# DeltaNet and MLP kernel: the first chunk's triangular inverse with 64-wide products and predicated evictions, later key norms read from the diagonal of K K^T, and an order planner that knows the port shared by VectorE and GpSimd

## The chip, the core and the metric

The kernel runs on one core of one Trainium2 chip. The metric is the device time of one execution in microseconds; lower is better. The engines are named as in the profile: PE (TensorE; PEld is its weight load), DVE (VectorE), ACT (ScalarE), POOL (GpSimd) and SP (SyncE, which here only issues DMAs). A name such as L841 is line 841 of the kernel before, unless the text says that it is the kernel after.

## The reference

Batch 4, 8 heads, 768 tokens, head size 48, all in float32. The first block is a delta-rule recurrence, the second a layer norm and a two-layer MLP with a residual:

```python
k_n = k / (np.linalg.norm(k, axis=-1, keepdims=True) + 1e-06)
state = np.zeros((B, H, D, D))
for t in range(S):
    y[:, :, t] = einsum('bhd,bhde->bhe', q[:, :, t], state)
    v_old = einsum('bhde,bhd->bhe', state, k_n[:, :, t])
    state = state + bt * einsum('bhd,bhe->bhde', k_n[:, :, t], v[:, :, t] - v_old)
...
x = y.transpose(0, 2, 1, 3).reshape(B, S, H * D)          # H * D = 384
xn = (x - mean) / sqrt(var + 1e-06) * g_ln
out = x + maximum(xn @ w_ch1, 0) @ w_ch2                  # 384 -> 1536 -> 384
```

The MLP weights are float64 in memory and are converted on the chip.

## The kernel before

**Tiling.** The sequence is cut into 12 chunks of C = 64 tokens, for all 32 (batch, head) pairs at once; two batches lie on each half of the 128 partitions. For a chunk, `gram` (L962) computes K K^T on TensorE, `queries` (L970) computes the masked product of q and k, and an inverse of a 64 x 64 unit triangular matrix per head (built from beta, the norms and K K^T) turns the recurrence into products. `recur` (L1127) multiplies it by v (for chunk 0 at L1173), scales the result to u (L1179), makes the output y (L1199), updates the state (L1209), and goes through the layer norm (`bn_stats` L1240, the root L1246, `xln` L1252) and a transpose (L1261) to xnt (L1265). `mlp(c)` (L1284) then does 12 first products of three k-tiles each (L1294), the relu eviction on ACT (L1302), the second product (L1310), the residual add to o on DVE (L1319) and the write.

**Three ways to the inverse.** Chunk 0 uses `first_inverse` (L813), doubling on TensorE: stage n multiplies a masked part of the scaled gram matrix with the inverse so far (product E, L876), evicts it, multiplies again (product Z, L893), transposes (L898) and copies back (`odd_back`, L801). It works on 32-column halves: four stages (n = 1 to 4) for the diagonal blocks of 32, whose masks are multiplied in beforehand (L860, seven on POOL and one on DVE), and a closing pair of products for the corner block (L906, L911). Its two halves of the heads, g = 0 and 1, alternate. Chunk 1 uses `rows_inverse` (L994) with blocks of FB = 16: it is a forward substitution on DVE, 15 steps of a multiply (L1025) and a subtract (L1030) with n * w elements, then a write of the result to memory (xd), eight loads into xt, and two joins of blocks on TensorE (`blocks_join` L1043, `join` L1078). Later chunks go in pairs through `rows_inverse` with blocks of BK = 32 and one `join`.

**Norms.** Chunk 0 has `first_norms`. For later chunks `norms` (L1112) squares k on ACT (L1115), reduces on DVE (L1116), takes three roots on ACT (L1117, L1120), adds 1e-6 on POOL (L1124) and scales v on POOL (`scale_v`, L773).

**Weights.** They come in 12 pieces through five buffers; `convert` (L656) takes each through ACT (L668, L683), DVE (shift L673, mask L678), POOL (multiply L688) and DVE (L700). The buffer of a piece is free for the next fetch after L700.

**Blocks.** `load_blocks` (L609) loads k or q of one chunk in eight DMAs of 32 x 32 blocks, `turned` (L930) transposes them on DVE (L933). `prep_g(m)` (L1390) does this for k of chunks 2m and 2m+1 and computes their grams.

**The order of the work.** Every operation is entered as a `Step` with an engine, a cost estimate and the keys that it reads and writes. `Line.run` (L204) simulates the engines with these costs and lists the steps; `emit` writes them in that order, and each engine executes its instructions strictly in it. DMAs stand in the order of the queue that issues them (SP, ACT or POOL). `pr` is a step's priority, `due` the wanted time of an MLP product; `PATIENCE` is how long an engine may be kept idle for an urgent step. The order is thus fixed when the kernel is built: a step that is late on the chip holds up all behind it on its engine.

Of the kernel before, what the change touches and what calls it, by code (L numbers as in the profile page):

```python
# [59 lines left out]
class Step:  # L60
    __slots__ = (
        "eng", "cost", "fn", "deps", "pr", "lag", "bulk", "start", "end", "n", "users", "name", "t0", "np", "arr", "hold", "ready", "least", "due"
# [3 lines left out]
class Line:  # L66
# [3 lines left out]
    HOP, GIVE, PATIENCE, SLACK, EAGER = 0.17, 0.1, 1.5, 3.0, 0.0  # L70
# [11 lines left out]
    def add(self, eng, cost, fn, r=(), w=(), pr=0.0, lag=0.0, bulk=None, name="", t0=0.7, after=(), np=0, arr=0.0, hold=None, due=None):  # L82
# [3 lines left out]
        s.hold, s.due = False, due  # L86
        deps = set()
# [100 lines left out]
    def foresee(self, now):  # L188

        soon, ends = {e: [] for e in ENGS}, {}  # L190
        for s in self.held:
            if s.start is not None:
                if s.end is not None:
                    ends[s] = s.end
                continue
            t = max(s.t0, now, s.least)
            for d in s.deps:
                z = d.end if d.end is not None else ends.get(d, now)
                t = max(t, z + (0.03 if d.eng == s.eng and d.bulk is None else self.HOP))
            ends[s] = t + s.cost + (self.PE_TAIL if s.eng == "PE" else 0.0)  # L200
            soon[s.eng].append((t, s))
        self.soon = {e: sorted(v, key=lambda x: x[0])[:6] for e, v in soon.items()}

    def run(self):  # L204
# [9 lines left out]
        self.held = [s for s in self.steps if s.hold]  # L214
        self.foresee(0.7)
# [3 lines left out]
        free = {e: 0.7 for e in ENGS}  # L219
# [9 lines left out]

        while todo:  # L230
            best = None
            for e in ENGS:
                for rd, s in self.avail[e]:
                    t = max(free[e], rd)
                    if s.bulk is not None:
                        x = lane(s, e)
                        if x is None:
                            continue
                        t = max(t, x)
                    if best is None or t < best[0]:  # L240
                        best = (t, e)
# [6 lines left out]
            for rd, s in self.avail[e]:  # L248
                if rd <= t + 1e-9:
                    if s.bulk is not None:  # L250
                        x = lane(s, e)
                        if x is None or x > t + 1e-9:
                            continue
# [14 lines left out]
            first = [max(r, t + 0.1) for r, h in self.soon[e] if h.start is None and h.pr < pick.pr]  # L268
# [11 lines left out]
            s.start = t  # L280
            todo -= 1
# [60 lines left out]
def kernel(  # L342
# [77 lines left out]
    masks = [sb(f"m{i}", [128, C], FP32 if i else I32) for i in range(6)]  # L420
    mask4 = sb("mask4", [128, BK], I32)
    xor, bits = sb("xor", [128, C], I32), sb("bits", [128, C], I32)
    eye = sb("eye", [128, BK])
    bm = sb("bm", [128, 2])
# [21 lines left out]
    gds = [dram.tile([128, GH, C], FP32, name=f"gd{i}") for i in range(NG)]  # L446
# [31 lines left out]
    def c_pool(fn, cost, w, r=(), pr=-200, **kw):  # L478
        add("Pool", cost, fn, r, w, pr=pr, hold=False, **kw)

    def c_dve(fn, cost, w, r=(), pr=-200, **kw):
        add("DVE", cost, fn, r, w, pr=pr, hold=False, **kw)

    for i in (0, 2, 1, 3):
# [4 lines left out]
    esx = pts[1]  # L489
    nought = esx.rearrange("p h t -> p (h t)")  # L490
    c_dve(lambda: nc.vector.memset(nought[:, 0:128], 0.0), 0.2, [("esx", 0), ("esx", 1)], pr=-300)
# [10 lines left out]
        lambda: nc.vector.tensor_scalar(  # L502
            out=xb[:, 0, 0:1].bitcast(I32), in0=xor[:, 0:1], scalar1=5, scalar2=1,
            op0=ALU.logical_shift_right, op1=ALU.bitwise_and,
        ),
        0.15, ["bma"], ["xor"],
    )
    for b in range(2):
        c_dve(
            lambda b=b: nc.vector.tensor_scalar(  # L510
                out=bm[:, b : b + 1], in0=xb[:, 0, 0:1].bitcast(I32), scalar1=b, scalar2=None, op0=ALU.is_equal
            ),
            0.15, [("bm", b)], ["bma"], pr=-199,
        )
    c_dve(
# [8 lines left out]
        lambda: nc.vector.tensor_scalar(out=flat[:, 960:992], in0=xor[:, 0:BK], scalar1=BK - 1, scalar2=None, op0=ALU.bitwise_and),  # L524
        0.17, ["eyx"], ["xor"],
    )
    c_dve(
        lambda: nc.vector.tensor_scalar(out=eye, in0=flat[:, 960:992], scalar1=0, scalar2=None, op0=ALU.is_equal),
        0.17, ["eye"], ["eyx"],
    )  # L530
    MPR = [-200, -200, -199, -198, -197, None, -196]
    for n in (0, 1, 2, 3, 4, 6):
        k_, m, w = min(n, 4) if n == 6 else n, masks[n] if n < 6 else mask4, C if n < 6 else BK
        t1, t2 = (flat[:, BK + C * i : BK + C * i + w] for i in (2 * n, 2 * n + 1))
# [4 lines left out]
            0.17, [("ma", n)], ["xor"], pr=MPR[n],  # L539
        )  # L540
        c_dve(
            lambda t2=t2, k_=k_, w=w: nc.vector.tensor_scalar(
                out=t2, in0=bits[:, 0:w], scalar1=k_, scalar2=1, op0=ALU.logical_shift_right, op1=ALU.bitwise_and
            ),
            0.18, [("mb", n)], ["bits"], pr=MPR[n],
# [5 lines left out]
            0.22, [("mask", n)], [("ma", n), ("mb", n)], pr=MPR[n],  # L551
        )
    MASK_SCRATCH = [(x, n) for x in ("ma", "mb") for n in (0, 1, 2, 3, 4, 6)] + ["bma", "eyx"]
    xc = us.rearrange("p h d -> p (h d)")[:, 0 : GH * BK].rearrange("p (h t) -> p h t", t=BK)
    c_pool(
        lambda: nc.gpsimd.tensor_copy(out=es, in_=eye[:, None, :].to_broadcast([128, GH, BK])),
        0.62, [("es", 0), ("es", 1)], ["eye"],
    )
# [72 lines left out]
    ON_DVE = ((1, 1),)  # L631
# [24 lines left out]
    def convert(i, c0=0, n=WN, **kw):  # L656
# [17 lines left out]
            wk, hk, **kw,  # L674
# [799 lines left out]
```

## Time and profile before

| what | value |
|---|---|
| median of 3 runs | 607.21 us (606.29 to 609.96) |
| the profiled execution's own time | 608.22 us |
| its span, first to last instruction | 606.5 us |
| mean granted TensorE clock | 0.946 |
| first MLP product (L1294) starts | 68.26 us |
| first E product of chunk 0's doubling (L876) starts | 15.45 us |
| first product with v (L1173) starts | 52.96 us |
| POOL mask multiplies (L860) | 7, 9.9 us |
| row result of chunk 1 written (xd) | 73.34 us |

The page of a profile gives, in its first part, the busy time and share of each engine; in its second the span in 40 equal slices, a digit being the busy share in tenths, with the granted TensorE clock below in the same tenths. A line of a list of waits reads "engine, tile and line, <- what ended the wait: us in total, times, longest". A line of the timeline starts with its start and its length in us. In a table of windows, each engine has busy us and, in brackets, instructions; at the end stand the clock, the DMA share and GB/s. A group line ends with busy us, mean ns of one, and the idle time before it with what ended it.

### The profile page before, as it was taken

To read this page: it belongs to the slowest core of one execution; us is meant where nothing else is said; L and a number is where in the kernel's file an instruction comes from. 1 tells how busy PE (TensorE), PEld (TensorE's weight loads), DVE (VectorE), ACT (ScalarE), POOL (GpSimd) and SP (SyncE) were. 2 spreads that over 40 slices of the span, in tenths; PEclk is the share of its full clock that TensorE was granted. 3 is DMA by queue.
4 is the path that set the end of the run, shared out by engine and by line. 5 is a ranking of instruction groups with operands and counts; after the bars stand their busy time and mean duration, and the time that the engine had idled before them with its cause. 6 is when DMAs were issued, how large, how long until landed. Compare 5 with 4: busy or idle time off the path is not lost.

```text
span 606.5 us, 20389 instructions
## 1 busy us (share of the span) xinstructions
PE 556.4 (92%) x9118; PEld 414.8 (68%) x9118; DVE 315.0 (52%) x709; ACT 171.9 (28%) x406; POOL 125.0 (21%) x164
## 2 busy tenths in 40 slices
PE   7855886999999999799989899998999999999996
PEld 4744665668678667568758577767768678677773
DVE  7876987994145981236970327951349814210000
ACT  5554564112142202232203223203314023221010
POOL 7784165623303130013130010100010000100000
PEclk9555697999999999999999999999999999999999
DMA  8981378877346343137243245031340030010101
GB/s 188 271 151 20 118 210 167 139 115 131 55 116 126 53 70 79 29 102 132 41 65 78 39 119 98 14 79 19 86 89 16 14 85 4 2 27 0 27 0 26
DMA packets 160039, 48.49 MB, mean 80 GB/s; under 512 B 151112, under 2 KB 154320, under 8 KB 159952
## 3 DMA queue, kind: packets, MB, share of 16 engines
q1 hardware_dynamic: 154064, 42.65, 33.5%
q0 software_dynamic: 2720, 3.96, 4.0%
q8 instruction: 71, 1.16, 0.8%
q10 hardware_dynamic: 3168, 0.59, 0.6%
q14 instruction: 16, 0.13, 0.1%
HBM read 33.93 MB, written 13.24 MB: 78 GB/s over the span
## 4 chain that ended last, share of the span: by engine, by line
PE 77%; DVE 11%; ACT 4%; issue 3%; DMA 3%; SPq 2%; ACTq 0%; DVEq 0%
PE ffa L1294 20%; PE ffa L1310 18%; PE ffb L1310 10%; PE ffb L1294 9%; PE two L950 3%; SPq L475 2%; PE ffb L1094 2%; PE by L1199 2%; DVE tmp L1025 2%; DVE xb L1030 2%; PE ffb L1089 2%; PE by L1139 2%; PE two L1192 2%; PE two L1209 1%; PE by L1261 1%
## 5 line engine op out<-in xcount | busy, mean ns | idle before, releaser
L1294 PE MATMUL ffa<-xnt,w_sb 128*128 128x256 f32 x600 | 148.8, 392 | 4.6 <-DVE o L1319 3.3
L1310 PE MATMUL ffa<-w_sb,h_all 128*128 128x384 f32 x384 | 146.0, 494 | 1.0 <-ACT h_all L1302 0.6
L1294 PEld LDWEIGHTS ffa<-xnt,w_sb 128*128 128x128 f32 x600 | 112.9, 194 | 29.1 <-DVE o L1319 7.3
L1310 PEld LDWEIGHTS ffa<-w_sb,h_all 128*128 128x128 f32 x384 | 70.1, 190 | 43.8 <-ACT h_all L1302 2.3
L1310 PE MATMUL ffb<-w_sb,h_all 128*128 128x384 f32 x192 | 79.2, 494 | 4.7 <-ACT es L1099 2.8
L1302 ACT ACTIVATE h_all<-ffa 128x256 f32<-128x256 f32 x100 | 35.7, 381 | 166.5 <-PE ffa L1294 112.0
L1294 PE MATMUL ffb<-xnt,w_sb 128*128 128x256 f32 x264 | 65.2, 383 | 1.7 <-ACT es L1099 1.4
L1030 DVE TENSOR_TENSOR xb<-xb,tmp 128x60 f32<-128x60 f32 (+19 forms) x170 | 60.6, 357 | 5.8
L1025 DVE TENSOR_TENSOR tmp<-xb,gb 128x60 f32<-128x60 f32 (+19 forms) x170 | 58.3, 343 | 4.0
L475 POOL DMA_DIRECT2D tb<-in_k_dram x80 | 52.2, 659 | 39.1 <-DVE kt L933 31.3
L1294 PEld LDWEIGHTS ffb<-xnt,w_sb 128*128 128x128 f32 x264 | 49.2, 190 | 10.5 <-ACT es L1099 2.0
L1310 PEld LDWEIGHTS ffb<-w_sb,h_all 128*128 128x128 f32 x192 | 35.0, 190 | 28.0 <-ACT es L1099 4.8
L1124 POOL TENSOR_SCALAR knrm<-knrm 128x16 f32<-128x16 f32 x11 | 3.7, 337 | 234.5 <-ACT knrm L1120 227.1
L1104 DVE COPY xt<-ffb 32x512 f32<-32x512 f32 x22 | 15.0, 684 | 53.3 <-PE ffb L1089 24.4
L1302 ACT ACTIVATE h_all<-ffb 128x256 f32<-128x256 f32 x44 | 16.9, 384 | 67.5 <-PE ffb L1294 61.3
L1082 DVE STREAM_TRANSPOSE xnj<-xt 128x512 f32<-128x512 f32 x11 | 7.8, 710 | 49.8 <-DMA xt<-xd 28.3
L1319 DVE TENSOR_TENSOR o<-ffa,x 128x384 f32<-128x384 f32 x16 | 8.8, 556 | 41.7 <-PE ffa L1310 37.0
L1319 DVE TENSOR_TENSOR o<-ffb,x 128x384 f32<-128x384 f32 x8 | 4.4, 552 | 41.2 <-PE ffb L1310 35.3
L688 POOL TENSOR_TENSOR words<-words,x 128x768 f32<-128x768 f32 (+1 forms) x11 | 20.0, 1821 | 21.3 <-ACT xnt L1265 8.8
L1099 ACT ACTIVATE es<-ffb 32x512 f32<-32x512 f32 x22 | 13.0, 589 | 38.0 <-DVE xt L1104 18.3
L933 DVE STREAM_TRANSPOSE qt<-tb 128x1024 f32<-128x1024 f32 x10 | 12.4, 1240 | 16.5 <-PE two L950 16.5
L1116 DVE TENSOR_REDUCE ksum<-xln 128x16 f32<-128x768 f32 x11 | 10.4, 949 | 19.2 <-ACT xln L1115 19.2
(169 smaller groups left out, 648.9 us busy)
## 6 DMA issues: line engine op xcount, KB each, us to landing
words<-in_moe_w_ch_dram SPq DMA_DIRECT2D x10, 768.0 KB, 5.8
gd<-gsb SPq DMA_DIRECT2D x11, 512.0 KB, 3.5
v<-in_v_dram SPq DMA_DIRECT2D x24, 192.0 KB, 3.9
kr<-in_k_dram SPq DMA_DIRECT2D x48, 96.0 KB, 3.3
out_dram<-o SPq DMA_DIRECT2D x48, 96.0 KB, 2.2
tb<-in_k_dram POOLq DMA_DIRECT2D x40, 64.0 KB, 3.3
gb<-gd SPq DMA_DIRECT2D x40, 64.0 KB, 3.7
tb<-in_q_dram SPq DMA_DIRECT2D x40, 64.0 KB, 2.9
```

Source lines behind the costliest of these rows:

```text
L475: add(eng, cost, lambda: QUEUE[eng].dma_start(out=out_, in_=in_), r, w, bulk=n * ns / 16e3, **kw)
L688: lambda: nc.gpsimd.tensor_tensor(out=lo.bitcast(FP32), in0=lo.bitcast(FP32), in1=esc.bitcast(FP32), op=ALU.mult),
L933: lambda: nc.vector.transpose(dst.rearrange("p i (u t) -> p i u t", t=BK), tb[i].rearrange("p (h u d) -> p h u d", u=2, d=BK)),
L950: nc.tensor.matmul(p_g[half(e ^ (hp & n)), hp, g * NP + j], kt[drows(hp), l], rt[drows(hp), i])
L1025: nc.vector.tensor_tensor(out=t, in0=xv[:, 0:n, j : j + 1].to_broadcast([128, n, w]), in1=gv[:, j : j + 1, j + 1 : L].to_broadcast([128, n ...
L1030: nc.vector.tensor_tensor(out=rest, in0=rest, in1=t, op=ALU.subtract)
L1099: add("ACT", act(512), lambda rows=rows: nc.scalar.mul(es[rows], p[rows], -1.0), [ATT[1]], [("es", e)], **kw)
L1104: "DVE", dve(512), lambda rows=rows: nc.vector.tensor_copy(out=xt[rows, :, BK:C], in_=p[rows]),
L1294: nc.tensor.matmul(p[:, 0:TOK], w1_sb[:, t, f * 128 : (f + 1) * 128], xnt[:, t], start=(t == 0), stop=(t == KC - 1))
L1302: "ACT", act(256), lambda hk=hk, p=p: nc.scalar.activation(h_all[:, hk], p[:, 0:TOK], ACTF.Relu),
L1310: lambda f=f, g=g, p=p, hk=hs[f]: nc.tensor.matmul(p[:, 0:DM], h_all[:, hk, g * 128 : (g + 1) * 128], w2_sb[:, f], start=(f == 0), stop=(f ...
L1319: lambda o=o, p=p, g=g: nc.vector.tensor_tensor(out=o, in0=p[:, 0:DM], in1=x[:, g], op=ALU.add),
```

## The change

1. `first_inverse` works on all 64 columns, in five stages (n = 1 to 5) and no closing pair. Product E (L851 after) multiplies the scaled gram matrix as it is, without a mask, with the transposed inverse so far. Its eviction is a `copy_predicated` on DVE (L859 after): only the elements that stage n's mask keeps are written, over an identity matrix that stands in the buffer beforehand. Product Z (L855 after) of that with the inverse so far is the new inverse; DVE transposes it (L866 after), and ACT copies it back in three pieces (L822 after; in the last stage one of the three is on DVE, L820 after).
2. POOL writes these six identity buffers before (L556 after, two copies of 512 each). They lie in buffers that chunks 1 to 3 use later (kt, two gsb, two xt, pt). The POOL mask multiplies are gone; there is one mask more (n = 5) to build on DVE.
3. The row steps of chunk 1's `rows_inverse` (blocks of 16) are on POOL; those of later chunks stay on DVE.
4. `norms` no longer squares and reduces: two DMAs on SP read the diagonal of K K^T of the chunk from memory (1024 single elements each), one root follows on ACT (L1064 after). For this the gram buffers in memory have one row more.
5. `prep_g(1)` loads its blocks (chunks 2 and 3) through SP instead of POOL; later ones stay on POOL.
6. The planner: steps carry `port`; a step of DVE isn't started while a POOL step with which it would share the port runs, and the other way round. PATIENCE is 0.8 instead of 1.5, the estimate of coming steps counts when an engine is free, and the MLP products' due times after chunk 0 are 6 us later. `hold=False` of the constants' helpers is dropped; `add` doesn't use the argument.

In the order that comes out, the DVE instructions of the doubling stand among the weight conversions as before; the transposes of k for chunks 2 and 3 (L873 after) stand ahead of chunk 0's xln; on TensorE the q transposes and `queries` of chunk 1 stand ahead of the transposes of xln; on ACT the root of chunk 1's norms stands between the two layer-norm roots of chunk 0. On SP, counted from the weight piece that SP issued at 14.13 us in the profile before, 51 DMAs stand ahead of the write of chunk 1's row result (the last of the moved block loads is the 41st); before there were 35.

```diff
-    HOP, GIVE, PATIENCE, SLACK, EAGER = 0.17, 0.1, 1.5, 3.0, 0.0
+    HOP, GIVE, PATIENCE, SLACK, EAGER = 0.17, 0.1, 0.8, 3.0, 0.0
...
+        s.port = port if eng != "Pool" else 1 if bulk is not None else port or 2
...
+            if s.port:
+                until, kind = ports["Pool" if e == "DVE" else "DVE"]
+                if kind + s.port > 2:
+                    t = max(t, until)
...
+    BEGIN = [(kts[2], "kt", 2), (gsbs[2], "g", 2), (gsbs[3], "g", 3), (xts[2], "xt", 2), (xts[3], "xt", 3), (pts[1], "pt", 1)]
+    for t, *key in BEGIN:
+        for g in range(2):
+            c_pool(
+                lambda t=t, g=g: nc.gpsimd.tensor_copy(out=t[:, g * H : g * H + H], in_=eye[:, None, :].to_broadcast([128, H, C])),
+                0.65, [(*key, x) for x in range(2)], ["eye"],
+            )
...
+        for n in range(1, 6):
+            ep, ekey = paired(BEGIN[n][0]), tuple(BEGIN[n][1:])
+            for g in range(2):
...
+                        nc.tensor.matmul(pe_[half(e), hp, j], gs[a, hp, j], xnj_[a, hp, j])
...
+                        nc.tensor.matmul(px[half(e ^ hp), hp, j], ep[half(e), hp, j], xt[half(e), 2 * j + hp])
...
+                    "DVE", 0.75,
+                    lambda i=i, n=n, ep=ep: nc.vector.copy_predicated(
+                        ep[:, :, i], masks[n][:, None, None, :].to_broadcast(shape), pe_[:, :, i]
+                    ),
...
+                if n < 5:
+                    add("DVE", dve(512), lambda i=i: nc.vector.transpose(xnj_[:, :, i], px[:, :, i]), Z, [("qt", 1, g)], **kw)
+                back(g, px, Z, ("ACT", "ACT", "ACT") if n < 5 else ("ACT", "DVE", "ACT"))
...
+        eng = nc.gpsimd if L < BK else nc.vector
...
-                nc.vector.tensor_tensor(out=rest, in0=rest, in1=t, op=ALU.subtract)
-
-            add("DVE", 2 * dve(n * w), row, gbk, ["xb"], **kw)
+                eng.tensor_tensor(out=rest, in0=rest, in1=t, op=ALU.subtract)
+
+            if L < BK:
+                add("Pool", 2 * (0.28 + 1.9e-3 * n * w), row, gbk, ["xb"], **kw)
+            else:
+                add("DVE", 2 * dve(n * w), row, gbk, ["xb"], port=1, **kw)
...
-        add("ACT", act(768), lambda: nc.scalar.square(ksq, kr), raw_keys(c), KSQ, **kw)
-        add("DVE", dve(768), lambda: nc.vector.tensor_reduce(out=ksum[i], in_=ksq, axis=AXX, op=ALU.add), KSQ, [("ks", i)], **kw)
...
+            own = flat[e * C * w : e * C * w + C * (w + 1)].rearrange("(s x) -> s x", x=w + 1)[:, 0:w:C]
+            dma("SP", ksum[i][half(e)], own, GH * C, 11, [("gd", c % NG)], [("ks", i, e)], **kw)
...
+        add("ACT", 0.22, lambda: nc.scalar.sqrt(knrm[i], ksum[i]), [("ks", i, e) for e in range(2)], kk, **kw)
...
-        return 42.0 + 42.2 * c + 1.35 * t - (14.0 if c else 0.0)
+        return 42.0 + 42.2 * c + 1.35 * t - (8.0 if c else 0.0)
...
-            load_blocks(2 * (c % 2), k, c, "Pool", pr=pr, t0=40.0 * m if m > 1 else 18.0)
+            load_blocks(2 * (c % 2), k, c, "Pool" if m > 1 else "SP", pr=pr, t0=40.0 * m if m > 1 else 18.0)
```

## The prediction

> **What bounds the kernel now.** I read the page first, then the windows by stage, the PE waits in the worst stage, and the timeline there. The page:
>
> ```profile
> span 606.5 us, 20389 instructions
> ...
> PE 556.4 (92%) x9118; PEld 414.8 (68%) x9118; DVE 315.0 (52%) x709; ACT 171.9 (28%) x406; POOL 125.0 (21%) x164
> ...
> PE   7855886999999999799989899998999999999996
> ...
> PEclk9555697999999999999999999999999999999999
> ```
>
> TensorE is the bound, but not from the start: its idle 50.1 us and its half clock lie mostly in the first eight slices (15.2 us each). By stage (PE busy is the second number):
>
> ```profile
> core 0: us, PE busy (x) PEld busy (x) DVE busy (x) ACT busy (x) POOL busy (x), PEclk, DMA share, GB/s
> 0.00:15.45 15.45, 11.77 (x163) 7.58 (x163) 11.57 (x48) 9.01 (x19) 11.91 (x27) 0.90 0.90 189
> 15.45:52.96 37.51, 23.94 (x717) 21.54 (x716) 27.57 (x51) 21.80 (x58) 25.70 (x30) 0.50 0.81 176
> 52.96:68.26 15.30, 9.49 (x207) 8.10 (x207) 12.42 (x41) 7.49 (x14) 4.50 (x4) 0.50 0.02 3
> 68.26:120.00 51.74, 43.69 (x1054) 33.72 (x1055) 44.06 (x78) 22.41 (x40) 29.30 (x29) 0.91 0.80 182
> 120.00:606.50 486.50, 467.49 (x6981) 343.80 (x6979) 219.40 (x495) 111.22 (x276) 53.63 (x76) 1.00 0.31 61
> ```
>
> The cuts are the first product of the doubling (15.45), the product with v (52.96), the first MLP product (68.26). So: 13.6 us idle in the doubling, 5.8 in the tail to the MLP, 8.1 in the middle, 19.0 later. After 68.26 TensorE has about 507 us of full-clock work (538.2 minus 27.1 idle minus 4.5 lost to half clock at 68.3 to 70.5 and 97.9 to 104.7). That work doesn't shrink, so **the change is worth the earlier MLP start plus the later stalls that it takes away**. Why the doubling is slow:
>
> ```profile
> PE two L876 <- ACT pt L880: 4.4, 2, 4.2
> PE by L893 <- ACT u L811: 4.0, 2, 2.7
> ```
>
> ```profile
> 12.04 2.33 DVE L841 COPY_PREDICATED es<-m,gsb 128x256 f32<-128x256 int32 x2
> 27.68 2.25 DVE L673 TENSOR_SCALAR words<-words 128x384 uint32<-128x384 uint32 x1
> 28.21 1.49 POOL L777 TENSOR_TENSOR v<-v,knat 128x768 f32<-128x768 f32 x1
> 35.35 1.14 PE L950 MATMUL ffb<-qt,kt 48*64 48x64 f32 x32
> 42.15 3.12 DVE L673 TENSOR_SCALAR words<-words 128x768 uint32<-128x768 uint32 x1
> ```
>
> ACT is named, but ACT's copy stood behind DVE: the L673 op takes 0.35 us alone (23.65) and 2.25 or 3.12 beside Pool work. A copy_predicated of 256 takes 0.45 alone, 1.08 and more beside Pool's mask multiply (L860).
>
> **What the Trainium skill says.** "GPSIMD Engine Reference", 8. Key points: GpSimd shares its SBUF interfaces with VectorE and contends with DVE instructions in a 2-port mode or with two SBUF inputs; the trace agrees (0.35 against 2.25). "TensorE: Matmul & The Clock Gate", Part 1: the clock is half or full, by activity over windows of about 3.4 us; here 1.00 to 12.5 us, 0.50 until 70.5. "DMA: Bandwidth & Descriptors", Why small descriptors are slow: a fixed cost per packet; the new norm transfers are 1024 elements of 4 bytes each, which no run here shows.
>
> **The change, part by part.**
>
> *Before the doubling.* Pool writes 12 identity copies of 512 (L556 shows one: 0.62), 7.4 us, about 5.4 to 14. They may delay the DVE norm chain (9.05 to 10.3): 0 to 2, I take 0.5. Against it the identity products (L849, 2 x 1.22) go, which stood before the first E. E of group 0 then starts at the end of the gram of chunk 1 (14.4) plus 0.5: about 15.0.
>
> *Doubling.* Before: four stages of E, Z with 32 columns (1.08 per 32 products) plus two 32-wide closing products per half. After: five stages, 4 x 32 products of 64 columns each. Price: the L950 row, 1.14 at half clock (the width costs 0.06, since the row of 32-wide ones is bound by issue). 20 x 1.14 = 22.8; four transposes and query halves between them, 4 x 1.11 = 4.4: 27.3 us of TensorE. DVE per stage: two predicated evictions from PSUM and two transposes of 512:
>
> ```profile
> L1082 DVE STREAM_TRANSPOSE xnj<-xt 128x512 f32<-128x512 f32 x11 | 7.8, 710 | 49.8 <-DMA xt<-xd 28.3 <-PE ffb L1089 21.5
> L1069 DVE COPY_PREDICATED xt<-mask,ffb 128x512 f32<-128x512 int32 x1 | 0.7, 719 | 0.0
> ```
>
> 2.86 a stage, under TensorE's 4.6, so hidden; uncovered it would be 14 us. ACT: six copies a stage at about 0.37 (L913 row), 2.2, hidden too. The seven Pool mask multiplies (9.9 us) are gone, and with them most of what held DVE up. Filling the pipe in stage 1, where each half waits for eviction and transpose: 3 us. Left-over waits, weight conversions being in DVE's and ACT's order as before: I take 2.7 of the former 13.6. v product at 15.0 + 27.3 + 3 + 2.7 = **48.0, against 52.96: -5.0**. If activity brings the clock back, 20 x 0.57 is saved in TensorE and DVE sets about 3.5 a stage: up to 6 us more. The window 12.5 to 15.9, equally dense with 64-wide products, didn't; so I don't count on it.
>
> *Rows of chunk 1 on Pool.* 15 steps of two ops leave DVE (about 0.4 a step, but the first step cost 2.85 at 56.3 and put u at 59.09, and steps stand between the layer-norm ops). On Pool a small tensor_tensor isn't shown; bounds: 0.21 (L1014) and 0.34 (L1124) each, plus 2.2 ns an element (1.85 for 768): 30 x 0.25 to 0.4, plus 2 x 680 elements x 2.2 ns = 3.0: 10.5 to 15. I take 11. Starting near 44, with a weight multiply and v scaling between: ends about 58, against 73.1. Hidden by the doubling's end and the tail. Queued behind them on Pool: the multiplies of weight pieces 3 to 5, due near 66.
>
> *Tail.* Walked with the rows of before: two products with v (2.2), u (0.55), y (1.1), copies, bn (to 5.8), rstd; then the order puts two transposes of k (2 x 1.24) on DVE ahead of xln, and the q transposes and queries of chunk 1 (2.2 each, half clock) on TensorE ahead of xln's transposes; xnt 15 us after the v product. Before 15.3: -0.3. The queries (L950 at 70.86, 1.16) are then already done: -1.2. MLP starts near **63, against 68.26**.
>
> *Middle, 68 to 120.* Idle 8.1 and clock loss 4.5. Its one big stall:
>
> ```profile
> ACT words L668 <- DMA words<-in_moe_w_ch_dram: 6.5, 2, 3.5
> ...
> PE ffb L1089 <- DVE xnj L1082: 5.1, 1, 5.1
> ```
>
> The join of chunk 1 stood on DVE behind conversions of weight pieces that waited for their DMA; the 5.1 us idle also brought the half clock. With the rows done 15 us earlier the join is due earlier relative to TensorE, but the new order still puts its predicated copy behind piece 9's shift, which waits for a buffer and 5.8 us of DMA. I take 8.1 of the 12.6 as staying: -4.5 (bounds 0 and -11).
>
> *Norms.* Each later chunk loses an ACT square (0.86), two of three ACT roots (0.2 each) and a DVE reduce (0.95); SP gains two DMAs (0.4 to 0.8 of issue). TensorE covers that already, so 0 by itself; less load on DVE and ACT shortens waits such as those on the o additions (10.6 us in the page's idle columns): -1.5, bounds -5 and +3, the planner's new order included.
>
> *Block loads of chunks 2 and 3.* 16 DMAs move from Pool (0.68 each) to SP, and two norm DMAs come before the row result. From 14.1 us on SP issues 51 ahead of the row result's write, against 35 before, 33 of them by 45.7. SP and POOL together issued 48 by 48.2: 0.71 each; SP alone 0.96 each. The last block load is the 41st; due 54.5 minus 3.3 landing, it fits at up to 0.90 each. I take 0.75: 0 cost; at 0.96 it is 2.3.
>
> *The planner's share.* `port` only orders DVE against Pool; its effect is in the left-over waits above. Dropping `hold=False` does nothing: `add` sets hold to False anyway.
>
> **Sum:** -5.0 - 0.3 - 1.2 - 4.5 - 1.5 = -12.5 on the span of 606.5: 594.0. The profiled execution took 608.2 (1.7 around its span), 1.0 over the median 607.2; so the median goes to 594.7, **595**.
>
> **Rivals.**
> 1. *Waits vanish or the clock warms (0.20).* For: Pool's multiplies go entirely, 64 columns double the array's work. Against: conversions still stand in the same queues. Doubling 6 us shorter, and of the middle's 8.1 only 5 left: 594.7 - 6 - 3.1 = 585.6; 576 to 588.
> 2. *Earlier start given back (0.16).* The MLP catches up with weight pieces whose DMA and conversion come no sooner. For: the DMA share is 0.80 in the middle, and the stall above hung on it. Then only the -1.2 and -1.5 stay: 604.5; 600 to 609.
> 3. *SP's queue becomes the wait; slower (0.14).* Block loads land late, DVE stands at the k transposes ahead of xln, the v scaling's root on ACT (it waits for the norm DMA) stands ahead of the second rstd, and the MLP starts late. The whole 12.5 us are lost when the pitch is (54.5 + 12.5 - 3.3 - 14.1)/41 = 1.21 us per DMA; the trace has 1.4 in one stretch (gb loads at 89.7). At 1.4 it is 14.1 + 57.4 + 3.3 = 74.8, 20.3 late, less 12.5: 615. Against: DMA is nearly idle from 46 to 68.
>
> **How the numbers follow.** The forecast's own band is 588 to 601 (0.50): left-over waits and middle stalls at their bounds. A measurement of this kernel tells about 1% from no change: faster means below 601.1, slower above 613.3. Faster: 0.50 + 0.20 + 0.02 of rival 2 = 0.72; same: 0.14 + 0.04 of rival 3 = 0.18; slower 0.10. Range 580 to 608: about 0.07 below, 0.12 above.
>
> **What would show it.** Right: no L860-like multiply on Pool, L859 evictions near 0.72, E/Z groups near 1.14 with few gaps, v product at 46 to 50, first MLP product at 60 to 65, rows' end on Pool before 60, idle between 63 and 120 below 10. Wrong: predicated copies above 1 us; Pool ops of the rows above 0.5; DVE waiting for tb loads at L873; TensorE waiting for weight pieces in the second half of the first MLP.

## The result and the profile after

The kernel after took 606.94 us (median of 12 runs, 605.54 to 608.75), the kernel before 608.03 on the same chip (605.18 to 611.36): ratio 0.9978, 95% interval 0.9957 to 0.9998. Ratios leave out runs over 1.5% above the fastest of the same kernel (here and below only two, 620.5 and 621.0 of e6), medians don't. The forecast was 595: nearly all of the expected gain is missing. The profiled execution took 606.63 us with a span of 604.6. The page of after, with the lines that answer to those of before:

```profile
span 604.6 us, 20327 instructions
...
PE 556.2 (92%) x9110; PEld 414.7 (69%) x9110; DVE 299.9 (50%) x667; ACT 156.8 (26%) x361; POOL 120.5 (20%) x182
...
PE   6757866999989999999999999999999999999996
...
PEclk9765887999999999999999999999999999999999
```

PE is busy as long as before (556.2 against 556.4), so what changed is idle time: 50.1 us before, 48.4 now. DVE lost 15 us of work, ACT 15, POOL 4.5, and it hardly shows. The windows of after, cut at the same events (first E product, bulk of the product with v, first MLP product, 120):

```profile
0.00:15.57 15.57, 9.81 (x159) 5.58 (x159) 13.59 (x44) 7.81 (x17) 12.95 (x33) 0.98 0.93 193
15.57:51.09 35.52, 22.95 (x714) 19.56 (x714) 21.90 (x48) 22.53 (x50) 11.54 (x18) 0.64 0.77 169
51.09:67.16 16.07, 11.74 (x268) 10.17 (x268) 12.96 (x25) 6.69 (x14) 10.79 (x27) 0.53 0.25 38
67.16:120.00 52.84, 41.60 (x982) 32.76 (x983) 32.68 (x52) 20.20 (x35) 32.91 (x33) 0.87 0.81 174
120.00:604.60 484.60, 470.12 (x6989) 346.62 (x6987) 218.78 (x503) 99.59 (x246) 52.34 (x73) 0.99 0.34 61
```

The first number after a window is its length, the second PE's busy time; their difference is idle time:

| stretch | idle before | idle after |
|---|---|---|
| to the first E product | 3.7 | 5.8 |
| doubling | 13.6 | 12.6 |
| tail to the MLP | 5.8 | 4.3 |
| middle, to 120 | 8.1 | 11.2 |
| from 120 on | 19.0 | 14.5 |

So the doubling is hardly denser, the MLP starts 1.1 us earlier (67.16 against 68.26) instead of 5.3, and the middle takes 3.2 back.

Why the doubling still waits is seen in its list of waits and in the timeline of one stage:

```profile
ACT xt L822 <- PE by L855: 8.6, 6, 2.5
DVE qt L866 <- ACT xt L822: 7.3, 6, 2.1
```

```profile
38.50 0.69 DVE L859 COPY_PREDICATED xt<-m,two 128x512 f32<-128x512 int32 x1
...
40.15 1.08 PE L855 MATMUL by<-xt,xt 64*64 64x64 f32 x32
40.44 0.73 DVE L859 COPY_PREDICATED xt<-m,two 128x512 f32<-128x512 int32 x1 [1.02 <-PE two L851]
41.36 0.72 DVE L866 STREAM_TRANSPOSE qt<-by 128x512 f32<-128x512 f32 x1 [0.19 <-PE by L855]
...
42.13 1.13 PE L855 MATMUL by<-xt,xt 64*64 64x64 f32 x32 [0.90 <-DVE nrm_b L947]
...
43.33 1.55 ACT L822 COPY xt<-by 128x256 f32<-128x256 f32 x4 [2.50 <-PE by L855]
...
44.91 0.72 DVE L866 STREAM_TRANSPOSE qt<-by 128x512 f32<-128x512 f32 x1 [2.10 <-ACT xt L822]
```

`by` and `two` are tiles in PSUM, the memory into which TensorE writes its products; each is [128, 2, 512] in the kernel, and the text calls each of the two parts of 512 columns a bank. Both halves of the heads (g = 0 and 1) have their Z products in both banks of `by`.

Each operation here costs what it was priced at (eviction and transpose near 0.72, products near 1.1; where the clock was up, products took 0.69). But the second half's Z product at 42.13, whose eviction ended at 41.17, starts only when the first half's transpose ends at 42.08, and the first half's copies on ACT start only after that product (43.26): the halves go through `by` one after the other, and so do its readers on ACT and DVE. The releaser named at 42.13, nrm_b, is only something that ended then. These waits are waits for semaphores of the program; whether the memory itself would demand them isn't told by any run here. The planner's keys name each half apart (`xk[g], xk[2 + g]`), so it counts the halves as independent, as the prediction did.

The longest single wait of PE in the doubling has another cause:

```profile
30.93 1.20 DVE L672 TENSOR_SCALAR h_all<-h_all 128x384 uint32<-128x384 uint32 x1
...
32.04 1.37 DVE L699 SCALAR_TENSOR_TENSOR w_sb<-h_all,scale_w 128x384 f32<-128x384 f32 x1
...
33.60 1.34 DVE L859 COPY_PREDICATED xt<-m,two 128x512 f32<-128x512 int32 x2
...
34.46 1.35 PE L855 MATMUL by<-xt,xt 64*64 64x64 f32 x64 [2.30 <-DVE xt L859]
```

The E products had ended at 32.17, and their evictions stood on DVE behind weight conversions until 33.60.

In the middle, PE waits for the relu on ACT, which stands behind a conversion that waits for its weight piece; lists of waits (66 to 125) and SP's timeline:

```profile
ACT words L667 <- DMA words<-in_moe_w_ch_dram: 8.6, 3, 4.3
...
PE ffa L1235 <- ACT h_all L1243: 6.8, 3, 3.6
```

```profile
85.89 1.66 SPq L488 DMA_DIRECT2D ksum<-gd  x2
87.60 6.41 SPq L488 DMA_DIRECT2D gb<-gd  x4
94.10 0.43 SPq L488 DMA_DIRECT2D words<-in_moe_w_ch_dram  x1
```

The piece fetched at 94.10 is p10, the fifth of the six late ones (87.45 before); the first of them, p6, was fetched at 71.83 (67.68 before). Ahead of p10 stand the transfers of the norms (ksum) and loads of K K^T blocks (gb). Before, the long wait of the middle was the 5.1 of L1089 on xnj; that one is down to 1.7.

### The profile page after: what moved, and what is told of

The parts are those of the page before. It is cut to its first block, busy times and chain, and to the rows that moved or that the text cites. A ratio compares the mean times of both kernels' runs of the same rounds, so it can differ in the third digit from the quotient of the medians.

```text
span 604.6 us, 20327 instructions
## 1 busy us (share of the span) xinstructions
PE 556.2 (92%) x9110; PEld 414.7 (69%) x9110; DVE 299.9 (50%) x667; ACT 156.8 (26%) x361; POOL 120.5 (20%) x182
## 4 chain that ended last, share of the span: by engine, by line
PE 75%; DVE 10%; ACT 4%; DMA 3%; SPq 3%; POOL 2%; issue 2%; ACTq 0%; DVEq 0%; POOLq 0%
PE ffa L1251 20%; PE ffa L1235 19%; PE ffb L1251 9%; PE ffb L1235 9%; PE two L890 3%; DMA words<-in_moe_w_ch_dram 3%; SPq L488 3%; PE by L1140 2%; PE ffb L1038 2%; PE ffb L1033 2%; PE two L1080 2%; PE by L1080 2%; PE two L1133 1%; PE by L1202 1%; ACT xt L822 1%
## 5 line engine op out<-in xcount | busy, mean ns | idle before, releaser
L1235 PE MATMUL ffa<-xnt,w_sb 128*128 128x256 f32 x600 | 150.5, 397 | 9.8 <-ACT h_all L1243 8.1
L1235 PEld LDWEIGHTS ffa<-xnt,w_sb 128*128 128x128 f32 x600 | 114.5, 196 | 34.2 <-ACT h_all L1243 12.3
L971 DVE TENSOR_TENSOR xb<-xb,tmp 128x31 f32<-128x31 f32 (+15 forms) x155 | 57.9, 374 | 5.3
L966 DVE TENSOR_TENSOR tmp<-xb,gb 128x31 f32<-128x31 f32 (+15 forms) x155 | 54.2, 350 | 4.4 <-POOL knrm L1065 0.5
L488 POOL DMA_DIRECT2D tb<-in_k_dram x64 | 41.6, 657 | 40.1 <-DVE kt L873 30.3
L873 DVE STREAM_TRANSPOSE qt<-tb 128x1024 f32<-128x1024 f32 x10 | 12.4, 1241 | 37.6 <-PE two L890 37.6
L1043 ACT ACTIVATE es<-ffb 32x512 f32<-32x512 f32 x22 | 13.0, 589 | 34.8 <-DVE xt L1048 16.1
L776 POOL TENSOR_TENSOR v<-v,knrm 128x768 f32<-128x768 f32 x11 | 17.1, 1556 | 9.3 <-DMA v<-in_v_dram 8.6
```

Source lines behind the costliest of these rows:

```text
L488: add(eng, cost, lambda: QUEUE[eng].dma_start(out=out_, in_=in_), r, w, bulk=n * ns / 16e3, **kw)
L776: lambda: nc.gpsimd.tensor_tensor(out=vs[c % 3], in0=vs[c % 3], in1=kn[:, :, None].to_broadcast([128, GH, D]), op=ALU.mult),
L966: eng.tensor_tensor(out=t, in0=xv[:, 0:n, j : j + 1].to_broadcast([128, n, w]), in1=gv[:, j : j + 1, j + 1 : L].to_broadcast([128, n, w]), ...
L971: eng.tensor_tensor(out=rest, in0=rest, in1=t, op=ALU.subtract)
L1235: nc.tensor.matmul(p[:, 0:TOK], w1_sb[:, t, f * 128 : (f + 1) * 128], xnt[:, t], start=(t == 0), stop=(t == KC - 1))
```

## Experiments

"Order kept" means that the planner is told the same steps as in the original, so that every engine's list of instructions is the same but for the edit. Where it isn't said, the planner planned anew. In diffs and timelines, "..." marks what is left out. Each ratio is to the kernel before on the same chip; that of the kernel after is 0.9978.

### The halves' banks

**e1_z_apart.**

```diff
+        pxs = (px, p_g)
...
-                E, Z = [ek[g], ek[2 + g]], [xk[g], xk[2 + g]]
+                E, Z = [ek[g], ek[2 + g]], list((xk, gk)[g])
...
-                        nc.tensor.matmul(px[half(e ^ hp), hp, j], ...)
+                        nc.tensor.matmul(pxs[g][half(e ^ hp), hp, j], ...)
```

The transpose and the copies back read `pxs[g]` too: the second half's Z products lie in the tile `ffa` instead of `by`. The planner found the same order with it.

> The kernel after with one edit: the Z products of the second half of the heads go to the two banks of ffa (idle until the MLP) instead of sharing by with the first half. Theory A (the halves wait for each other because they share banks): TensorE's idle time in the doubling, 12.6 us in the kernel after, falls to about 6; the product with v comes 4 to 6 us sooner than 51.1, at 45 to 47. Rival B (DVE and ACT with their weight conversions set the pace): idle time stays at 11 to 13, the product with v at 50 to 52. For the end: if the first MLP's late weight pieces take everything back, the time stays within 1.5 us of the kernel after (606.9); if they don't, it falls by 4 to 6.

Measured: 600.72 us, ratio 0.9883 (0.9862 to 0.9904), about 6 us below the kernel after. The product with v starts at 46.4 (its very first instruction in after: 50.3), the MLP at 62.4. Timeline of e1 at the same kind of place:

```profile
32.97 1.13 PE L856 MATMUL by<-xt,xt 64*64 64x64 f32 x32 [2.65 <-DVE xt L860]
...
33.84 1.11 PE L856 MATMUL ffa<-xt,xt 64*64 64x64 f32 x32
34.21 0.37 ACT L823 COPY xt<-by 128x256 f32<-128x256 f32 x1 [0.62 <-PE by L856]
34.62 0.72 DVE L867 STREAM_TRANSPOSE qt<-by 128x512 f32<-128x512 f32 x1 [1.18 <-ACT xt L823]
...
35.75 0.71 DVE L867 STREAM_TRANSPOSE qt<-ffa 128x512 f32<-128x512 f32 x1
```

The second Z product follows the first at once, and the copies begin while it runs. Theory A holds for the times, not for its idle figure. The doubling, up to the very first product with v, in after and then in e1:

```profile
15.50:50.30 34.80, 22.54 (x712) 19.30 (x713) 21.95 (x48) 22.24 (x49) 10.93 (x15) 0.65 0.78 173
15.50:46.40 30.90, 20.94 (x713) 18.32 (x714) 21.95 (x48) 22.35 (x50) 10.33 (x13) 0.67 0.84 190
```

Of the 3.9 us gained, 2.3 are idle time (12.3 to 10.0) and 1.6 PE's busy time. The 10.0 that stay are far above theory A's 6. ACT and DVE still take turns within one half (34.21, 34.62): the lists of e1 have 4.4 and 4.2 us of such waits left. And the eviction behind weight conversions is still there, 2.65 us at 32.97: rival B has a part. The gain itself is no accident of one execution: in six kernels that keep the order and share `by` (e9, e12, e13, e14, e15, e17) the product with v starts at 50.5 to 51.5, in e18, the other one with Z apart, at 45.5. As e1 gives the second half both another tile and other banks, it doesn't tell which of the two the waits hang on.

**e16_e_apart.** The same edit for E instead of Z (`pes = (pe_, p_g)`), order kept.

> The kernel after with its order kept, the E products of the second half of the heads in the two banks of ffa instead of sharing two with the first half; the Z products stay in by. If the shared banks of E hold the doubling up as those of Z did: the product with v 2 to 4 us sooner than 50.3, the time 2 to 5 below the kernel after. If the chain goes over the Z banks, where one half's products wait for the other's transpose and copies on two engines: under 1.5 us.

Measured: 605.01, ratio 0.9962 (0.9941 to 0.9984); the product with v at 49.8 (50.3 in after). The interval overlaps that of the kernel after: at most a small part. What sharing costs, it costs at Z.

### One part at a time, planned anew

**e2_old_norms, e3_rows_dve, e6_pool_loads, e4_old_doubling, e5_old_planner.** The edits: `norms` of before; in `rows_inverse`

```diff
-        eng = nc.gpsimd if L < BK else nc.vector
+        eng = nc.vector
```

with the step entered for DVE; in `prep_g`

```diff
-            load_blocks(2 * (c % 2), k, c, "Pool" if m > 1 else "SP", ...)
+            load_blocks(2 * (c % 2), k, c, "Pool", ...)
```

the doubling and masks of before in the kernel after; the `Line` class and due times of before in the kernel after.

> The kernel after with the norms of the later chunks as in the kernel before (ACT square, DVE reduce, three ACT roots, no norm transfers). Theory C (the 4-byte norm transfers on SP, 1.7 us of issue each at chunk 2 and a write of K K^T waited for before them, stand ahead of the weight pieces p8 to p11): those pieces are fetched 2 to 6 us sooner, idle time from 67 to 120 falls from 11.2 to 8 or less, and the time by 2 to 4 us unless the steady state loses it again. Rival D (fewer operations on ACT and DVE are what the steady state gained): idle time from 120 on rises from 14.5 towards 19, and the time rises by 2 to 5.

Measured: 606.82, ratio 0.9987 (0.9971 to 1.0004), not to be told from the kernel after. (The 1.7 us of issue that were expected for each norm transfer at chunk 2 are those of two, 85.89 above.)

> The kernel after with the rows of chunk 1's 16-wide inverses on DVE again. Theory E (on Pool they took 18.3 us in place of 11 and held the third operation of weight pieces 4 and 5 back, and with them the buffers and fetches of the next pieces): the pieces from p6 on are fetched 2 to 4 us sooner, idle time from 67 to 120 falls by 2 to 4, time down 1 to 4. Rival (DVE, which carries the layer norm and the conversions, gets the 8 us back): product with xln later than 67.2 by 2 to 4, the time up 1 to 4.

Measured: 608.76, ratio 1.0022 (1.0009 to 1.0036).

> The kernel after with the 16 block loads of chunks 2 and 3 on Pool's queue again. If their place on SP delays the weight pieces behind them (rival 3 of the prediction in a mild form): pieces from p6 on are fetched 2 to 4 us sooner and the time falls by 1 to 4. If SP has room for them: the time stays within 1 us, or rises by 1 to 2 since Pool issues them (0.68 us each) beside its identity copies and the rows of chunk 1.

Measured: 615.29, ratio 1.0105 (1.0072 to 1.0137), by the ratios about 8 us above the kernel after, more than any theory gave.

> The kernel before with everything of the change but the doubling and its masks (norms from the diagonal, rows on Pool, block loads on SP, the new planner). If the new doubling is worth what its own stretch shows (1.9 us at the product with v), the time is 1 to 3 us above the kernel after, 608 to 610. If the first MLP waits for its weight pieces whatever comes before, it is within 1 us of the kernel after. If the new doubling's Pool copies, banks and 64-wide products cost as much as they save, it is 1 to 3 us below, 604 to 606.

Measured: 615.4, ratio 1.0142 (1.0112 to 1.0172), again outside all. Its product with v starts at 48.8, earlier than in before and after; the loss comes after it (the MLP at 67.6, idle 12.1 and clock 0.80 from there to 120).

> The kernel after with the planner of the kernel before (no shared port between DVE and Pool, patience 1.5, due times 14 before their line instead of 8, its look ahead at waiting producers as before); doubling, norms, rows and block loads stay. The kernel before with everything but the doubling measured 615.4, 8 above the kernel before. Theory F (the new planner's order costs these 8: it fills TensorE's tail and the middle with work of later chunks): the time falls by 3 to 8 against the kernel after, to 599 to 604, and idle time from 67 to 120 falls from 11.2 to below 8. Rival G (norm transfers, block loads and rows cost them, not the planner): the time stays at 605 to 609. If the planner's port was a gain, it rises to 609 to 613.

Measured: 617.0, ratio 1.0172 (1.0142 to 1.0202). Above all three expectations: theory F isn't borne out, but see e11 below.

Four of five leave-one-out kernels are slower than the kernel after, two by about 8 us and one by 10, for parts of quite different weight. That looked less like prices than like the planner's order. Two tests:

**e11_nudged_planner.**

```diff
-    HOP, GIVE, PATIENCE, SLACK, EAGER = 0.17, 0.1, 0.8, 3.0, 0.0
+    HOP, GIVE, PATIENCE, SLACK, EAGER = 0.18, 0.1, 0.8, 3.0, 0.0
```

> The kernel after with one constant of the planner changed by a hundredth of a microsecond (the time it reckons from one engine to another, 0.17 to 0.18): no operation changes, only the order that the planner finds. Theory J (the order is a draw: any small change of costs makes another one, and the leave-one-out runs e3 to e8 show draws rather than prices): the time moves by more than 3 us either way, most likely up, to 610 to 617. Rival K (the parts have their prices and the planner is stable): it stays at 605 to 608.5.

Measured: 612.72, ratio 1.0088 (1.0056 to 1.012). No operation changed, and about 6 us came on. Theory J holds.

**e12_pool_loads_same_order.** The edit of e6 with the order kept: only the queue that issues the 16 loads differs.

```diff
-        add(eng, cost, lambda: QUEUE[eng].dma_start(...), ...)
+        add(eng, cost, lambda: QUEUE[via or eng].dma_start(...), ...)
...
-            load_blocks(2 * (c % 2), k, c, "Pool" if m > 1 else "SP", ...)
+            load_blocks(2 * (c % 2), k, c, "Pool" if m > 1 else "SP", via="Pool", ...)
```

> The kernel after with its order kept, but the 16 block loads of chunks 2 and 3 issued by Pool at the places where SP had them. With the planner planning anew this edit cost 8.4 us. If that was the new order: within 2 us of the kernel after. If the loads on Pool are themselves the price (0.68 us each beside the rows of chunk 1, which end later, and the join with them): 611 or more.

Measured: 607.43, ratio 1.0 (0.9986 to 1.0013). The edit that cost about 8 us planned anew costs 0.5 with the order kept (1.3 by the ratios). So e2 to e6 are no prices of the parts, and from here on the order is kept.

### What the weight pieces take

**e7_no_late_weights_after, e8_no_late_weights_before** (planned anew), **e9_no_late_weights_same_order_after, e10_no_late_weights_same_order_before.**

```diff
-        fetch(i, pr=i)
-        convert(i)
+        dst, key = pieces[i][0], pieces[i][3]
+        add("DVE", dve(768), lambda dst=dst: nc.vector.memset(dst, 0.01), [], [key + (x,) for x in range(2)], pr=5.0 + i)
```

All four leave out the fetch and conversion of pieces 6 to 11, so their output isn't that of the reference. In e9 and e10 the steps are entered as before, with nothing behind them but the memset in the place of the last.

> The kernel after, with weight pieces 6 to 11 (all of the second MLP matrix) neither fetched nor converted: six memsets of 768 on DVE put a constant there, so the output isn't that of the reference. Theory H (the first MLP waits for weight pieces; what is gained ahead of it is paid back there): idle time and half clock between 67 and 120 go nearly away, 8 us and more off the end, and against the same cut of the kernel before the gain shows, 4 us or more. Rival I (the middle waits for the chain of chunk 1, its rows, join and products): less than 4 us off, and no more gain against the same cut of before than 2.

Measured: 616.92, ratio 1.0161 (1.0126 to 1.0195): with less work, 10 us slower. Its order puts the product with v at 57.5.

> The kernel before with the same cut as e7_no_late_weights_after (weight pieces 6 to 11 replaced by memsets, output not that of the reference). Theory H: it loses its idle time of 8.0 and its half clock between 68 and 120 too, 8 us or more off, and ends 4 us or more above the same cut of the kernel after. Rival I: it ends within 2 of it.

Measured: 599.95, ratio 0.9883 (0.9848 to 0.9918). Beside e7 this says nothing of the pieces, as e9 shows.

> The kernel after with its order of instructions kept (the planner is told the same steps), but with nothing issued for the fetch and conversion of weight pieces 6 to 11; where the last operation of each stood, a memset on DVE fills the matrix, so the output isn't that of the reference. The two cuts before this one let the planner plan anew and showed mostly its new order. Theory H (the middle waits for weight pieces): of the 11.2 us of idle time and about 5 us of half clock between 67 and 120, 8 or more go, and the time falls to 599 or less. Rival I (the chain of chunk 1 and the order of TensorE's queue hold it): it falls by 4 at most, to 603 or more.

Measured: 594.52, ratio 0.9785 (0.9754 to 0.9815).

> The same cut of the kernel before, its order kept (weight pieces 6 to 11 replaced by memsets, output not that of the reference). Its middle lost 8.0 us idle and some 4 of clock. Theory H: 6 or more go, to 601 or less, and the same cut of the kernel after ends at least 2 below it, by its earlier MLP start. Rival I: 605 or more.

Measured: 599.71, ratio 0.987 (0.9843 to 0.9898). The middle of e9, and then of e10:

```profile
67.80:120.00 52.20, 49.56 (x1177) 38.14 (x1180) 32.56 (x63) 11.31 (x27) 24.10 (x29) 0.91 0.68 112
```

```profile
68.40:120.00 51.60, 48.61 (x1205) 37.10 (x1206) 39.25 (x78) 14.22 (x34) 18.45 (x26) 0.99 0.58 107
```

Idle falls to 2.6 and 3.0. Theory H holds: the late pieces, with their fetches, conversions and waits, cost 12.4 us in the kernel after (606.94 to 594.52) and 8 in the kernel before. Without them the change is worth 5.2 us (599.71 to 594.52, on the same chip, intervals apart), with them 1. About 4 us of gain are lost at the pieces.

### What makes the pieces dearer than before

**e13_rows_dve_same_order.** `eng = nc.vector` as above, the steps left where they were.

> The kernel after with its order kept, but the two operations of each row step of chunk 1 issued on DVE at the place where Pool had them. Theory E (the rows stand ahead of the multiply of weight piece 3 on Pool, which ran from 67.33 although its input was there near 64; p6's buffer, fetched at 71.83, comes free only then): p6 is fetched 2 to 4 us sooner and the time falls by 2 to 4, to 603 to 605, if DVE takes the 30 small operations without delaying the layer norm. Rival L (they delay DVE's conversions and layer norm by as much): within 1.5 us, the first MLP product later than 67.2.

Measured: 611.6, ratio 1.0074 (1.0056 to 1.0093). p6 is fetched at 77.26 rather than 71.83. Rival L: on DVE, at these places, they delay more. The other remedy, the weight multiply ahead of the rows on POOL, wasn't tried.

**e14_norm_transfers_twice.**

```diff
+                nc.sync.dma_start(out=kspare[half(e)], in_=own)
```

> The kernel after with its order kept and every norm transfer issued twice, the second into a spare tile (22 more transfers of 1024 elements of 4 bytes). Theory C (these transfers delay SP's queue and the weight pieces): p10 and p11 are fetched 1 to 3 us later, the time rises by 1 to 3. Rival M (SP's stall at that place comes from the loads of K K^T blocks, and DMA has room): within 1 us.

Measured: 615.91, ratio 1.0141 (1.0117 to 1.0166): 9 us, more than expected.

```profile
87.94 4.32 SPq L1066 DMA_DIRECT2D ksum<-gd  x1
...
104.24 0.75 SPq L489 DMA_DIRECT2D words<-in_moe_w_ch_dram  x1
```

A norm transfer behind the added ones holds SP for 4.32 us; p10 is fetched at 96.62, 2.5 later than in after, p11 (the second line) 4.9 later. The 4.32 can't be put down to the doubled number: in e12, with the single set, one such transfer held SP for 4.31 us, at the time of the kernel after. So e14 shows what more transfers cost, not how.

**e17_no_norm_transfers_same_order.** The same transfers left out (`skip=True`), a constant in their place.

> The kernel after with its order kept and no norm transfer issued; the roots of the later chunks read a constant, so the output isn't that of the reference. Theory C (the transfers stand in SP's queue ahead of p10 and p11, and the copies in e14 cost 9 us for twice as many): p10 is fetched 2 to 5 us sooner than 94.1, idle time from 67 to 120 falls from 11.2 by 3 to 5, the time falls by 4 to 9, to 598 to 603. Rival M' (SP's stall there comes from the block loads of K K^T, which come one after the other anyway; e14 overloaded the queue): within 2 us, 605 to 608.

Measured: 604.53, ratio 0.9958 (0.9941 to 0.9976), 1 to 2.4 us below the kernel after by ratio and by median; the intervals overlap. SP's timeline:

```profile
85.25 6.04 SPq L490 DMA_DIRECT2D gb<-gd  x5
91.39 0.44 SPq L490 DMA_DIRECT2D words<-in_moe_w_ch_dram  x1
```

p10 comes 2.7 us sooner, and p11 (96.72) 2.7. PE's wait for the relu falls from 6.8 to 2.5, idle in the middle from 11.2 to 6.6. Most of that doesn't reach the end: PE's busy time is 3.4 us longer at a lower mean clock (0.938 against 0.95), and from 120 on there are 15.8 us idle instead of 14.5. The first set is cheaper than the second one was; the block loads' six microseconds stay without it (Rival M' in part).

**e15_fetches_first.** In `emit`, each fetch of p6 to p11 goes right behind the last step that it depends on:

```diff
+            out.remove(s)
+            out.insert(max(out.index(d) for d in s.deps) + 1, s)
```

> The kernel after with its order kept but for SP: the fetches of weight pieces 6 to 11 are put directly behind the step that frees their buffer, ahead of some block loads of K K^T, result writes and loads of v. p10 was fetched 4.9 us and p11 4.6 us after their buffers came free, p7 2.0. Theory C' (their place in SP's queue is what delays the middle): p10 and p11 come 2 to 5 us sooner, ACT's wait for words falls from 8.6 to below 6, the time falls by 2 to 4, to 603 to 605. Rival (the conversions behind them on DVE, ACT and Pool stay where they are in the order, and what is moved back on SP is late in turn): within 1.5 us.

Measured: 608.26, ratio 1.0019 (0.9986 to 1.0051): no gain. p10 came only 1.7 sooner (92.43) and p11 0.8 later (100.21), so the edit moved too little to judge theory C' (the place of the fetches in SP's queue as the price).

**e18_z_apart_norms_by_pool.** e1 with `via="Pool"` at the norm transfers.

> The kernel of e1 (Z products of the two halves in banks of their own, order as in the kernel after) with the norm transfers issued by Pool at the same places of the order. If their place in SP's queue is the price: p10 sooner than e1's 87.97 by 2 to 5 us, the time 2 to 6 below e1's 600.7. If the transfers' own packets are the price, or Pool's wait for the write of K K^T holds the weight multiplies up in its turn: 599 to 604.

Measured: 601.83, ratio 0.9904 (0.9878 to 0.9931), not to be told from e1. p10 is fetched at 83.91 (e1: 87.97), 4 us sooner as theory C would have it, and idle in the middle is the same, 7.5 us: there the time of p10's fetch alone set nothing. Of the kernels that leave nothing out, e1, at 0.9883, is the fastest, with e18 beside it.

## Why the prediction was wrong, point by point

The span was forecast at 594.0 and was 604.6. Of these 10.6 us, 4.2 arose before the first MLP product (67.16 for 63) and 6.4 after it. With Z apart (e1) the span is 597.6: 7.0 of the 10.6 come back, 4.8 of them before the first MLP product.

- **First E product, 15.0:** 15.57. Nearly right.
- **Doubling, the failed step of the first part.** "Filling the pipe in stage 1 ... 3 us" and "Left-over waits ... I take 2.7" allowed 5.7 us of idle time; it was 12.6. PE's own 27.3 us were in turn too much (22.95: the clock was partly up, 0.64 instead of 0.50). The prices of eviction and transpose were right. What failed was the sentence that DVE's 2.86 us and ACT's 2.2 a stage are "hidden": it took for granted that one half computes while the other is evicted. Where they share `by` they go one after the other. e1 shows this for 3.9 us of the doubling, 2.3 of them idle. The other 10.0 us of idle time were not taken apart by experiment; the trace shows among them the turns of ACT and DVE within a half and evictions behind conversions. That e1's product with v comes at 46.4 (forecast 48.0) and its MLP at 62.4 (forecast 63) is in part luck: its idle time is 4.3 above what was allowed, and PE's work 6.4 below its price.
- **Conversions in DVE's queue**, named for the left-over waits, did hold PE up: 2.30 us at 34.46, and 2.65 in e1, nearly all of the 2.7 by itself.
- **Tail, -0.3 and -1.2:** 16.1 us instead of 15.0; the shift of k's transposes and chunk 1's queries went as walked.
- **Rows on POOL, 11 us, from near 44 to 58:** they ran from 49.09 to 67.38, 18.3 us:

```profile
55.41 1.01 POOL L687 TENSOR_TENSOR h_all<-h_all,x 128x384 f32<-128x384 f32 x1 [2.29 <-DVE x L677]
...
60.87 0.31 POOL L966 TENSOR_TENSOR tmp<-xb,gb 128x63 f32<-128x63 f32 x1
...
63.64 0.46 POOL L966 TENSOR_TENSOR tmp<-xb,gb 128x48 f32<-128x48 f32 x1
...
67.33 3.66 POOL L687 TENSOR_TENSOR words<-words,x 128x768 f32<-128x768 f32 x2
```

  The 30 operations themselves took 9.9 us, so their price was about right. They began 5 us later than assumed, and in between stood a weight multiply that waited 2.29 us for its input, and the norm and scaling of v. Some of the last ones were slow: one of 48 elements took 0.27 at 51 us and 0.46 at 63.64, beside DVE's weight conversions, while the one at 60.87 kept its 0.31 beside DVE's transposes of k. The prediction named what was queued behind (the multiplies of pieces 3 to 5) and gave them no price: they started at 67.33, and p6's buffer came free at 71.8.
- **Middle, -4.5, the failed step of the second part:** idle rose by 3.2, and the mean clock fell from 0.91 to 0.87. The prediction counted the one named stall and put the waits for the weight pieces as unchanged. The named stall (join behind the shift) did shrink, from 5.1 to 1.7; a wait for the relu behind the conversions took its place (1.2 before, 6.8 after): by way of ACT, the last of the listed signs of being wrong, TensorE waiting for weight pieces. e9 and e10 put the loss at the pieces.
- **Norms and the rest, -1.5:** idle from 120 on fell by 4.5. That it was the norms is only argued; e11, with the same operations, had 17.4 there.
- **Block loads, 0:** right (e12).

Of the rivals, the second (the earlier start given back at the weight pieces, 604.5, range 600 to 609) came closest in time and place. Its reason, "weight pieces whose DMA and conversion come no sooner", is only half of it: the pieces are no fixed wall. In e1 they are fetched 4.8 to 6.1 us sooner (67.03 for p6, 93.25 for p11), as their buffers come free behind the doubling and the rows, and the earlier MLP start (4.8 us) reaches the end in full. The third rival (SP's block loads late ahead of xln) didn't occur. What stays open: which part made the pieces dearer. The norm transfers' share in time isn't certain (e17, e18), the rows' place on POOL was only seen in the trace (e13 moves them to where it is worse), and both hang on an order that the planner draws.

## What to carry to other kernels

When two interleaved halves are counted as hiding each other, look at what they share: a buffer with readers on two engines put the halves one after the other, though evictions and transposes cost what they were priced at. Where a planner writes the order, a part's price can only be measured with the order kept; one planned anew mixes it with a draw of several microseconds (e11: about 6, with no operation changed). When a step is moved in front of another on a queue, price the one behind it and the buffer that it frees.

## What the runs showed of the hardware beyond what was expected

- Small operations on POOL (tensor_tensor of 15 to 64 elements a partition) took 0.22 to 0.32 us, also beside DVE's transposes of k (0.31 at 60.87), 0.38 beside the layer norm's xln (61.64), and 0.43 to 0.50 beside DVE's weight conversions (62.5 to 66.8 us).
- A transfer of 1024 single elements holds SP's queue for 0.58 us at the least, 0.67 at the median and up to 2.24 in the kernel after. The longest one varies with the same number of transfers: 3.92 in e1, 4.31 in e12, and 4.32 in e14, which has twice as many.
- The clock of TensorE came up in the doubling for a while (mean 0.64, PE busy 65% of the stretch); before, with mostly 32-wide products, it stayed at 0.50 with PE busy 64%. What made the difference isn't shown.
